# A hand-placed order for attention and a channel mixer on one core: new order lists, q of four pairs scaled on ScalarE, two more weight chunks split on GpSimd

## The chip, the cores and the metric

One core of a Trainium2 chip runs the whole program in one launch. The metric is the device time of the program in microseconds (us). Engines are named as in the profile: PE is TensorE's matmul and PEld its weight load, DVE is VectorE, ACT is ScalarE, POOL is GpSimd, SP is SyncE, which here only issues DMAs.

## What is computed

```python
def _attn_ref(q, k, v, tau):                     # q, k, v: 8 x 8 x 576 x 64, f32
    scores = np.matmul(q, k.transpose(0, 1, 3, 2)) / np.sqrt(64)
    thresh = np.max(scores, axis=-1, keepdims=True) - tau
    scores = np.where(scores >= thresh, scores, -1e9)
    scores = scores - np.max(scores, axis=-1, keepdims=True)
    attn = np.exp(scores)
    attn = attn / (np.sum(attn, axis=-1, keepdims=True) + 1e-09)
    return np.matmul(attn, v)

def _moe_ref(x, w_theta, w_tok_r, w_tok_i, w_ch):  # x: 8 x 576 x 512, the attention's output
    theta = x @ w_theta
    zr, zi = x * np.cos(theta), x * np.sin(theta)
    y = np.einsum('ts,bsd->btd', w_tok_r, zr) + np.einsum('ts,bsd->btd', w_tok_i, zi)
    u = x + y
    return u + np.maximum(u @ w_ch, 0.0)
```

## The kernel before, in words

**Work.** There are 8 batches with 4 pairs of heads each, 32 pairs in all, numbered n. A pair has five units (L782): a unit takes 128 queries of both heads (the fifth the last 64 of each) through the scores on PE (L800, into PSUM banks), a copy out of PSUM with the row's extreme on DVE (L821), the threshold (a small addition on DVE, L831), the mask and the exponential with its sum on ACT (L845, L852) and a transposition in 32x32 blocks on DVE (L864, L866) into the pair's one buffer `a`. When all five have been transposed, `values` (L870) multiplies `a` with v on PE in 32-row tiles, in two halves (L881), and `divide` (L901) divides by the sums, which go through DRAM to be spread over the partitions.

After the four pairs of a batch comes `mixture` (L954): four products with w_theta (`angle`, L1002; PE L989), sines and cosines on ACT (L1085 to L1092), products with x on POOL or DVE (L1107), transpositions on PE (`flip`, L1122; L1132) and splits into a high and a low part (ACT L1138, DVE L1157), four products with the token weights (`token`, L1165; PE L1177), and four products with w_ch (L989 again). Matmuls of the mixture, and from pair 5 on the scores, take each operand as a high and a low part of a faster number type, in three products.

**Weights.** At the start, and for w_ch after the first batch's angles, `convert` (L555) splits chunks of 128 weight rows into the two parts. The chunks have numbers, `turn`: 0 to 3 are w_theta, 4 to 12 the nine chunks of w_tok, 13 to 16 w_ch. Its steps run on ACT (L581), POOL or DVE (L586), DVE (L600, L607, L614), then the low word: for a turn under `WORD_POOL` (L617) a cast (L621) and a product (L626) on POOL, in two halves each, else one operation on DVE (L633). Three matmuls (L650 to L652) sum the pieces up, and ACT copies the low part out (L656).

**q.** From pair 5 on (`WHOLE`), q is scaled on DVE (L726) and split into parts (L735 or L737, and the subtraction of `low`, L533). Pairs 1 to 4 use q whole: a DMA, then one scaling in place on POOL (L713). Pair 0 is scaled while its scores are copied.

**Order.** Nothing in the source is run where it stands. Every operation is entered in a `Plan` (L367) with its engine, and a list `ORDER`, written into the source, says in which order they are issued: each number is the step from the last operation's number to the next one's. Operations are numbered as the source creates them. One engine's instructions run in the order of the list; between engines only semaphores order them. `PLACES` names the buffer (of the 2 to 8 of its class) that each tile takes. The costs at each operation (`c_mm`, `c_act`, ...) and the due times (`AT`, `key`) were the planner's when it made the list; at run time they have no effect. SP issues all loads and stores but the first, in the list's order.

Of the kernel before, what the change touches and what calls it, by code (L numbers as in the profile page):

```python
# [64 lines left out]
        "0101201010110202100121021000211021201210210221010210210210201212011201"  # L65
    ),
    "xl": (
        "001201021001210230101032112030123102330121023102320130213210301232103012310231023"
    ),
    "xh": (  # L70
        "10321001322310322301021301320112012301023102130123102310231203012320130123102310232013012320131023"
    ),
    "rb": (
        "010101100010010110010000001000100010011000000111"
    ),
    "bank": (
        "33223267764546646774760404044034404043040404500000055467544657764774657375646745766545767644400000700000"
        "04000000700000056774567464565436746547566646776656740000007000000600000060000007757665675476537467546457"
        "67675574767500000040000006000000600000046774564657647556564775467676765757640000007000000700000070000004"
        "67546754767543677674457466645646675700000060000005000000700000057665574674546775575466746545656774670000"  # L80
        "00600000060000007000000476567456724347567657774565676767574500000060000006000000500007463776246534567327"
        "334566772367324567"
    ),
    "z": (
        "1021210212001200120012001200120012001200101"
    ),
    "q": (
        "01012310213021302130213021302130213021302130213021302130213"
# [8 lines left out]
        "10231230231020310201230132012030321002311302101233203201232102103121032021032031012032110213022130102130"  # L97
        "13202130012302103012302301103201320012102301103210321230111023013202103102101230013203120232100132210310"
        "23110320123010320123012202102301321031201320012301230132003120120310213213010230"
    ),  # L100
    "nm": (
        "01210100120101020010021011001010010010101001010201201010101010010100121001001010010101001001010100101001"
        "01021001010010101001010210010100101010010200101001110100"
    ),
    "s2": (
        "01201012100120110202102012010001201100101001001201010101001010020010110101001101102011001010010100100112"
        "00120101010010101001001201010101000101010010100120010010"
    ),
    "rows": (
        "01001001010101010000010101010101"  # L110
# [5 lines left out]
        "01234560231450623145026431524063"  # L116
# [8 lines left out]
        "1023012301200213012010210132020101200120010201320123010201321203"  # L125
    ),
    "zl4": (
        "1023012301201203012301230132023101320123012301320123013201321302"
    ),
    "zh1": (  # L130
        "01010000010101010001010101000110"
    ),
    "zl1": (
        "01010001010101010101010101010110"
    ),
    "rawq": (
        "011010111001010101100101100"
# [164 lines left out]
WORD_POOL = 10  # L302
# [1051 lines left out]
```

## Time and profile before

| | us |
|---|---|
| median of 3 runs | 912.23 (912.0, 912.23, 917.48) |
| profiled execution | 910.66 |
| its span, first to last instruction | 908.9 |
| operations in the order list: PE, DVE, ACT, POOL, SP | 1370, 1244, 1040, 426, 292 |

The profile is of one execution. An engine is busy while one of its instructions runs; matmuls are pipelined and overlap, so a busy PE may still be slower than it could be. "Idle before" names what ended a pause of an engine, taken from the semaphores; "issue" is a pause that no semaphore explains. "L800" is line 800.

### The profile page before, as it was taken

To read this page: it belongs to the slowest core of one execution; us is meant where nothing else is said; L and a number is where in the kernel's file an instruction comes from. 1 tells how busy PE (TensorE), PEld (TensorE's weight loads), DVE (VectorE), ACT (ScalarE), POOL (GpSimd) and SP (SyncE) were. 2 spreads that over 40 slices of the span, in tenths; PEclk is the share of its full clock that TensorE was granted. 3 is DMA by queue.
4 is the path that set the end of the run, shared out by engine and by line. 5 is a ranking of instruction groups with operands and counts; after the bars stand their busy time and mean duration, and the time that the engine had idled before them with its cause. 6 is when DMAs were issued, how large, how long until landed. Compare 5 with 4: busy or idle time off the path is not lost.

```text
span 908.9 us, 33820 instructions
## 1 busy us (share of the span) xinstructions
PE 860.7 (95%) x14542; PEld 771.0 (85%) x14542; DVE 714.4 (79%) x1571; ACT 692.2 (76%) x1394; POOL 341.0 (38%) x432
## 2 busy tenths in 40 slices
PE   5787999999999989999999989999999999999898
PEld 3565898898998989888999979998889888999898
DVE  7999969988569887788788876788787886876452
ACT  6788998767987689766997679866888669975550
POOL 2677543133445234234432433534234433421210
PEclk9899999999999999999999999999999999999999
DMA  6576352465213644235233452415433352424502
GB/s 254 183 233 227 105 177 95 140 209 204 92 56 118 220 157 153 88 103 175 103 134 112 149 195 92 156 46 193 159 128 118 104 181 89 136 68 138 181 1 76
DMA packets 62374, 126.13 MB, mean 139 GB/s; under 512 B 22512, under 2 KB 31632, under 8 KB 58128
## 3 DMA queue, kind: packets, MB, share of 16 engines
q1 hardware_dynamic: 62080, 123.97, 40.6%
q8 instruction: 114, 1.87, 0.8%
q14 instruction: 36, 0.29, 0.1%
q10 hardware_dynamic: 144, 0.00, 0.0%
HBM read 110.17 MB, written 13.78 MB: 136 GB/s over the span
## 4 chain that ended last, share of the span: by engine, by line
PE 62%; DVE 23%; ACT 7%; issue 4%; DMA 2%; POOL 1%; SPq 1%; DVEq 0%; POOLq 0%; ACTq 0%
PE banks_ps__66 L1177 20%; PE banks_ps__66 L989 14%; PE banks_ps__66 L881 13%; PE banks_ps__66 L800 10%; DVE sc L821 8%; DVE a L864 4%; PE banks_ps__66 L1132 3%; ACT s L852 2%; ACT sc L845 2%; DVE nm L831 2%; DVE xl L533 1%; DVE xh L607 1%; DVE a L866 1%; ACT ang L1023 1%; PE banks_ps__66 L650 1%
## 5 line engine op out<-in xcount | busy, mean ns | idle before, releaser
L845 ACT ACTIVATE sc<-sc,nm 128x576 f32<-128x576 f32 x288 | 217.1, 771 | 78.3 <-DVE nm L831 75.5
L852 ACT ACTIVATE s<-sc,small 128x576 f32<-128x576 f32 x288 | 222.7, 774 | 5.0 <-DVE a L866 0.2
L821 DVE TENSOR_SCALAR_CACHE_REDUCE sc<-banks_ps__66 128x576 f32<-128x576 f32 x279 | 199.7, 743 | 13.2 <-PE banks_ps__66 L800 11.6
L864 DVE STREAM_TRANSPOSE a<-s 128x576 f32<-128x576 f32 x256 | 187.3, 758 | 26.4 <-PE banks_ps__66 L881 18.9
L800 PE MATMUL banks_ps__66<-k,q 64*128 64x288 f32 (+1 forms) x1638 | 176.6, 326 | 17.4 <-DVE sc L821 11.7
L881 PE MATMUL banks_ps__66<-a,v 32*64 32x144 f32 x9216 | 168.6, 288 | 12.8 <-issue 7.1
L989 PE MATMUL banks_ps__66<-xh,wm 128*128 128x288 f32 x1024 | 171.9, 304 | 3.7 <-issue 1.4
L800 PEld LDWEIGHTS banks_ps__66<-k,q 64*128 64x128 f32 (+1 forms) x1638 | 134.0, 188 | 45.6 <-DVE sc L821 22.6
L881 PEld LDWEIGHTS banks_ps__66<-a,v 32*64 32x64 f32 x9216 | 148.4, 132 | 27.2 <-issue 15.9
L1177 PE MATMUL banks_ps__66<-wt_h,zh 128*128 128x288 f32 x576 | 160.8, 304 | 0.9 <-ACT zh L1138 0.8
L1177 PE MATMUL banks_ps__66<-wt_l,zh 128*128 128x288 f32 x576 | 161.6, 303 | 0.0
L989 PEld LDWEIGHTS banks_ps__66<-xh,wm 128*128 128x128 f32 x1024 | 144.9, 190 | 17.2 <-issue 11.0
L1107 POOL TENSOR_TENSOR z<-z,xT 128x288 f32<-128x288 f32 x112 | 89.3, 832 | 100.8 <-ACT z L1088 100.8
L1177 PEld LDWEIGHTS banks_ps__66<-wt_h,zh 128*128 128x128 f32 x576 | 108.0, 189 | 4.2 <-issue 2.9
L1177 PEld LDWEIGHTS banks_ps__66<-wt_l,zh 128*128 128x128 f32 x576 | 108.3, 189 | 2.6 <-issue 2.3
L533 POOL TENSOR_TENSOR xl<-xT,xh 128x288 fp32r<-128x288 f32 x78 | 67.4, 886 | 98.8 <-ACT xh L948 39.5
L533 POOL TENSOR_TENSOR k<-rawk,k 128x288 fp32r<-128x288 f32 x54 | 47.5, 890 | 139.4 <-ACT k L763 69.8
L1177 PE MATMUL banks_ps__66<-wt_h,zl 128*128 128x288 f32 x576 | 96.6, 302 | 0.0
L989 PE MATMUL banks_ps__66<-xl,wm 128*128 128x288 f32 x512 | 94.2, 301 | 1.7 <-DVE xl L533 1.6
L1157 DVE TENSOR_TENSOR zl<-banks_ps__66,zh 128x512 fp32r<-128x512 f32 (+1 forms) x96 | 51.1, 548 | 50.9 <-ACT zh L1138 50.6
L533 POOL TENSOR_TENSOR q<-rawq,q 128x320 fp32r<-128x320 f32 x54 | 48.2, 906 | 97.9 <-ACT q L737 44.6
L1177 PEld LDWEIGHTS banks_ps__66<-wt_h,zl 128*128 128x128 f32 x576 | 81.7, 188 | 2.9 <-issue 2.7
(82 smaller groups left out, 1022.7 us busy)
## 6 DMA issues: line engine op xcount, KB each, us to landing
v<-in_vp_dram SPq DMA_DIRECT2D x32, 1152.0 KB
wm<-wm_dram SPq DMA_DIRECT2D x64, 512.0 KB
out_dram<-xT SPq DMA_DIRECT2D x31, 288.0 KB
rawq<-in_qT_dram SPq DMA_DIRECT2D x27, 320.0 KB
rb<-sums_dram SPq DMA_DIRECT2D x64, 128.0 KB
rawk<-in_kT_dram SPq DMA_DIRECT2D x27, 288.0 KB
z<-in_w_tok_dram SPq DMA_DIRECT2D x9, 576.0 KB
wm_dram<-rb SPq DMA_DIRECT2D x16, 256.0 KB
```

The lines of the kernel that those rows point to most:

```text
L533: eng.tensor_tensor(out=out()[:, c0:c1], in0=in0()[:, c0:c1], in1=in1()[:, c0:c1], op=ALU.subtract)
L800: nc.tensor.matmul(ps()[:, 2 * j + h, :HS], q[a]()[r, i * P : (i + 1) * P], k[c]()[r, h * HS : (h + 1) * HS], start=(x == 0), stop=(x == l ...
L821: lambda j=j, sc=sc, scaled=scaled: nc.vector.tensor_scalar(out=sc().rearrange("p (a b) -> p a b", a=2), in0=ps()[:, 2 * j : 2 * j + 2, :H ...
L845: lambda j=j, sc=sc: nc.scalar.activation(out=sc(), in_=sc(), func=AF.Prelu, bias=nm()[:, 2 + j : 3 + j], scale=-1.0, alpha=STEEP),
L852: lambda j=j, sc=sc, total=total, weights=weights: nc.scalar.activation(out=weights(), in_=keys(sc()), func=AF.Exp, bias=back, accum_out=p ...
L864: nc.vector.transpose(out=a()[:, :, j, 32 * i : 32 * i + 32], in_=src.rearrange("p (c q) -> p c q", q=32))
L881: nc.tensor.matmul(ps()[64 * h : 64 * h + 64, b, :w], v()[r, c, h, :], a()[r, c, h, :], start=(c == 0), stop=(c == 17))
L989: nc.tensor.matmul(ps[h]()[:, :HS], wm()[:, a, c, :], parts[c][bb]()[:, h * HS : (h + 1) * HS], start=first and n == 0, stop=final and n = ...
L1107: eng.tensor_tensor(out=zi, in0=zi, in1=x[m]()[:, c0:c1], op=ALU.mult)
L1132: nc.tensor.transpose(out=tp()[:, i * P : (i + 1) * P], in_=z()[:, c : c + P], identity=ident)
L1157: lambda zh=zh, zl=zl, tv=tv: nc.vector.tensor_tensor(out=zl(), in0=tv(), in1=zh().bitcast(F32), op=ALU.subtract),
L1177: nc.tensor.matmul(ps()[:, :HS], zz[c][lo]()[:, zz[c][2]], w[:, c, hs], start=(q + n == 0), stop=(q + n == len(work) - 1),)
```

## The change

PLACES and ORDER are replaced throughout; PLACES keeps its classes and sizes. `WORD_POOL` goes from 10 to 12, so turns 10 and 11 (the seventh and eighth chunk of w_tok) take their low words on POOL. The scaling of q of pairs 1 to 4 moves from POOL to ACT. A branch for the threshold's addition on ACT is added, which `ADD_ACT = 0` never takes. The new list has 1370, 1242, 1044, 430 and 292 operations.

```diff
 PLACES = {
     "wm": (
-        "0101201010110202100121021000211021201210210221010210210210201212011201"
+        "0101201201021020121020201212010210201201202012021002101201011221021021"
     ),
...
 ORDER = (
-    "202 1 -203 200 1 4 2 -206 205 -204 8 39 159 1 1 5 1*4 -202 -13 -1 2 1 207 12 1 25 -244 5 241 -32 14 -15 92 -90 "
...
 TWICE = 5
 WHOLE = 5
+ADD_ACT = 0
 HI_POOL = 8
-WORD_POOL = 10
+WORD_POOL = 12
...
             if n:
-                gps(
-                    c_pool(QS) * 0.5, lambda: nc.gpsimd.tensor_scalar(out=q(), in0=q(), scalar1=gate, scalar2=None, op0=ALU.mult), key,
+                act(
+                    c_act(QS, ptr=True), lambda: nc.scalar.activation(out=q(), in_=q(), func=AF.Copy, scale=gate), key,
                     ((q, 0), small_b), ((q, 0),),
                 )
...
         over = [(nm, list(heads)), small_b]
-        dve(
-            0.15,
-            lambda: nc.vector.tensor_scalar(out=nm()[:, 2 : 2 + w], in0=nm()[:, :w], scalar1=cut, scalar2=None, op0=ALU.add),
-            t0 + A("add", n), over, ((nm, 2),), small=True,
-        )
+        if n < ADD_ACT:
+            act(
+                0.22, lambda: nc.scalar.activation(out=nm()[:, 2 : 2 + w], in_=nm()[:, :w], func=AF.Identity, bias=cut),
+                t0 + A("add", n), over, ((nm, 2),),
+            )
+        else:
+            dve(
+                0.15,
+                lambda: nc.vector.tensor_scalar(out=nm()[:, 2 : 2 + w], in0=nm()[:, :w], scalar1=cut, scalar2=None, op0=ALU.add),
+                t0 + A("add", n), over, ((nm, 2),), small=True,
+            )
```

## Rows read from the trace of the kernel before

**Rows 1.** The page, busy time of each engine, share, instructions.
```profile
PE 860.7 (95%) x14542; PEld 771.0 (85%) x14542; DVE 714.4 (79%) x1571; ACT 692.2 (76%) x1394; POOL 341.0 (38%) x432
```
**Rows 2.** Stretches: length, busy us by engine, PE clock, DMA share, GB/s.
```profile
0.00:23.00 23.00, 12.58 (x54) 7.74 (x56) 16.95 (x47) 15.98 (x32) 6.11 (x14) 0.92 0.69 251
23.00:46.00 23.00, 17.68 (x429) 13.12 (x432) 22.04 (x49) 17.87 (x37) 14.68 (x23) 0.87 0.57 181
46.00:68.00 22.00, 19.29 (x377) 13.41 (x367) 21.40 (x46) 19.16 (x41) 15.48 (x24) 0.91 0.77 239
68.00:91.00 23.00, 17.92 (x327) 12.95 (x317) 22.83 (x48) 19.98 (x44) 16.32 (x27) 1.00 0.67 226
...
91.00:909.00 818.00, 793.21 (x13411) 723.83 (x13394) 631.22 (x1384) 619.20 (x1244) 288.42 (x346) 1.00 0.39 129
```
**Rows 3.** The page, chain that ended last, by engine.
```profile
PE 62%; DVE 23%; ACT 7%; issue 4%; DMA 2%; POOL 1%; SPq 1%; DVEq 0%; POOLq 0%; ACTq 0%
```
**Rows 4.** Waits of PE over the span: us, times, longest.
```profile
PE banks_ps__66 L800 <- DVE sc L821: 11.7, 10, 3.3
...
PE banks_ps__66 L881 <- issue: 7.1, 7, 2.1
...
PE banks_ps__66 L989 <- issue: 1.4, 1, 1.4
```
**Rows 5.** Timelines of PE and PEld (start, us, what, idle before), and chain.
```profile
425.46 0.49 PE L881 MATMUL banks_ps__66<-a,v 32*64 32x144 f32 x13 [1.10 <-issue]
...
517.78 0.83 PEld L800 LDWEIGHTS banks_ps__66<-k,q 64*128 64x128 f32 x12 [0.17 <-issue]
...
525.21 0.49 PE L881 MATMUL banks_ps__66<-a,v 32*64 32x144 f32 x10 [2.14 <-issue]
...
159.01 2.40 PE banks_ps__66 L1177 x18
161.42 2.44 PE banks_ps__66 L881 x144
```
**Rows 6.** DMA queue, kind, packets, MB, share of 16 engines.
```profile
q8 instruction: 114, 1.87, 0.8%
```
**Rows 7.** Groups by line: busy us, mean ns, idle before.
```profile
L713 POOL TENSOR_SCALAR q<-q,small 128x640 f32<-128x640 f32 x4 | 7.7, 1923 | 0.0
...
L737 ACT CAST q<-rawq 128x640 fp32r<-128x640 f32 x14 | 10.1, 725 | 0.0
...
L1088 ACT ACTIVATE z<-z,small 128x576 f32<-128x576 f32 x32 | 24.6, 770 | 0.2
...
L1090 ACT ACTIVATE z<-z 128x576 f32<-128x576 f32 x32 | 21.4, 669 | 0.0
...
L621 POOL CAST xh<-z 128x288 fp32r<-128x288 uint32 (+1 forms) x16 | 8.0, 498 | 1.8 <-PE banks_ps__66 L651 1.6 <-PE banks_ps__66 L650 0.2
...
L626 POOL TENSOR_TENSOR xh<-xh,xl 128x288 fp32r<-128x288 f32 (+1 forms) x20 | 16.4, 830 | 9.1 <-DVE xl L614 8.3 <-DVE nm L831 0.5
```
**Rows 8.** Timeline of PE, 16 to 23 us.
```profile
16.89 1.24 PE L800 MATMUL banks_ps__66<-k,q 64*128 64x288 f32 x8 [1.06 <-POOL q L713]
21.44 1.81 PE L800 MATMUL banks_ps__66<-k,q 64*128 64x288 f32 x6 [3.31 <-DVE sc L821]
```
**Rows 9.** Timelines of DVE and POOL, 91 to 99 us.
```profile
91.59 0.74 DVE L633 SCALAR_TENSOR_TENSOR xh<-z,xl 128x576 fp32r<-128x576 uint32 x1
...
93.71 0.79 DVE L633 SCALAR_TENSOR_TENSOR xh<-z,xl 128x576 fp32r<-128x576 uint32 x1
...
97.93 1.14 DVE L633 SCALAR_TENSOR_TENSOR xh<-z,xl 128x576 fp32r<-128x576 uint32 x1
...
96.52 0.95 POOL L533 TENSOR_TENSOR k<-rawk,k 128x288 fp32r<-128x288 f32 x1 [2.63 <-DVE k L761]
```
**Rows 10.** Stretches after the start-up, columns as in rows 2.
```profile
91.00:100.00 9.00, 9.00 (x279) 7.61 (x264) 8.42 (x17) 8.80 (x20) 3.98 (x5) 1.00 0.11 24
100.00:110.00 10.00, 9.06 (x57) 7.48 (x54) 9.93 (x21) 9.25 (x22) 8.58 (x10) 1.00 0.28 73
```

More of the change, by code (lines that the diff above doesn't have):

```diff
@@ L64 @@
     "wm": (
-        "0101201010110202100121021000211021201210210221010210210210201212011201"
+        "0101201201021020121020201212010210201201202012021002101201011221021021"
     ),
     "xl": (
-        "001201021001210230101032112030123102330121023102320130213210301232103012310231023"
+        "002132012001210232010120301231023012302130123103210233012102301321023310201320123"
     ),
     "xh": (
-        "10321001322310322301021301320112012301023102130123102310231203012320130123102310232013012320131023"
+        "10031212030321031302312002231013020123201312032013120302131203102312030123120301231023021312030123"
     ),
     "rb": (
-        "010101100010010110010000001000100010011000000111"
+        "010101010110010101010000011101110111010000100110"
     ),
     "bank": (
[L77 to L82, printed above, removed]
+        "33356732676565745767460044044430004402440404700000033276547655765774637567457447765746757467400000400000"
+        "05000000600000067646757647545667765756475546756646460000004000000700000040000004577465746452736546753576"
+        "44564747674500000050000007000000600000066774564765754766546677566446674675470000007000000300000050000006"
+        "67657476543256747654575676476746576400000050000004000000500000067664574675675646746765763456567646750000"
+        "00400000040000007000000467457657664457637465675674464765563600000070000004000000700003235673564323472367"
+        "352465577546733526"
     ),
     "z": (
-        "1021210212001200120012001200120012001200101"
+        "0210210201201200120012001200120012001200101"
     ),
     "q": (
-        "01012310213021302130213021302130213021302130213021302130213"
+        "01201312030120312031203120312013201230123012301230123012301"
     ),
@@ L96 @@
     "sc": (
-        "10231230231020310201230132012030321002311302101233203201232102103121032021032031012032110213022130102130"
-        "13202130012302103012302301103201320012102301103210321230111023013202103102101230013203120232100132210310"
-        "23110320123010320123012202102301321031201320012301230132003120120310213213010230"
+        "10102323120132003112300321303120123021033012310321023012031032021301032012300123031200123013200123130210"
+        "13202103102303102103202103012313021103201230012030123200123102120310231102312103012301203012301302010210"
+        "32101321031210021230123201021310320130221012023110320123001123012010230210310230"
     ),
     "nm": (
-        "01210100120101020010021011001010010010101001010201201010101010010100121001001010010101001001010100101001"
-        "01021001010010101001010210010100101010010200101001110100"
+        "00112012001010210010201010101201012010120101010010120101001010010210120101010010100102000120101010100101"
+        "02001010010100102001020110100101010101010100012001020010"
     ),
     "s2": (
-        "01201012100120110202102012010001201100101001001201010101001010020010110101001101102011001010010100100112"
-        "00120101010010101001001201010101000101010010100120010010"
+        "00112012001021001120102101002101101101011020110210100100101010001010120121001010011010120101120101020120"
+        "10110110121100100120101201101201001001101010011001010112"
     ),
     "rows": (
-        "01001001010101010000010101010101"
+        "01000010010100100101010000100010"
     ),
@@ L115 @@
     "xT": (
-        "01234560231450623145026431524063"
+        "01234560123540613524160532416052"
     ),
@@ L124 @@
     "zh4": (
-        "1023012301200213012010210132020101200120010201320123010201321203"
+        "0120102301200102012012010132013201230102010101200120213001020102"
     ),
     "zl4": (
-        "1023012301201203012301230132023101320123012301320123013201321302"
+        "0132012301230123012301230132013201230132012301230123103201320132"
     ),
     "zh1": (
-        "01010000010101010001010101000110"
+        "01010000010100010100000001010101"
     ),
     "zl1": (
-        "01010001010101010101010101010110"
+        "01010100010101010101010001010101"
     ),
     "rawq": (
-        "011010111001010101100101100"
+        "010100010101011001100000101"
     ),
```

259 rows, old and new, of the table ORDER are left out of this document.

## The prediction

> **What bounds the kernel now.** I read the busy shares first. TensorE (PE) is busy 95% of the span, VectorE (DVE) 79%, ScalarE (ACT) 76%, GpSimd (POOL) 38% [rows 1]. So the end is set by PE's work plus the time in which PE stands, and an engine beside PE counts only where PE waits for it. Where PE stands is read from the table by stretches [rows 2]. From 0 to 91 us PE is busy 12.58 + 17.68 + 19.29 + 17.92 = 67.5 us, so 23.5 us are idle; from 91 us to the end it is busy 793.21 of 818 us, so 24.8 us are idle. In the second to fourth of the early stretches DVE is busy 22.04 of 23, 21.40 of 22 and 22.83 of 23 us: the start-up is bound by DVE. The chain of work that ended last agrees: PE 62%, DVE 23%, ACT 7%, "issue" 4% [rows 3]. Last, the waits name what ends PE's idle time [rows 4]: 11.7 us end with DVE emptying a score bank, 8.5 us (7.1 in seven stops within the products with v, 1.4 in one elsewhere) end with "issue", that is with nothing the profile shows.
>
> The stops by "issue" are what the word "segments" in the change is about. In the timeline a half of 144 of these matmuls breaks off after 131, 1.10 us pass, and the last 13 follow with no other engine named; another half breaks off after 134 for 2.14 us [rows 5]. The queue marked "instruction" moved 114 packets and 1.87 MB [rows 6], 16.4 KB each; PE runs 14,542 matmuls and as many weight loads [rows 1], together 29,084, which is 113.6 times 256. So PE's program comes in 114 pieces of 256 instructions, and a piece can be late.
>
> **The change part by part.** The order lists can be counted without running anything: each step of ORDER is the number of the next operation in the order in which the source creates them.
>
> *Scaling q of pairs 1 to 4.* POOL loses 4 x 1.923 = 7.7 us [rows 7]. ACT gets four operations that no row shows. The nearest is its cast of the same 128x640 tile, 0.725 us; a pointer operand costs 0.10 us on the sine (0.770 against 0.669) [rows 7], so I take 0.83 each, 3.3 us in all. What it can give: in the one place where PE waited for this operation, 1.06 us [rows 8]. But 4.5 us later PE stands again, 3.31 us for DVE [rows 8], whose queue is no shorter. I take 0, with bounds of -1.1 us and of +3.3 us (all four in the way of the softmax; ACT is busy 53.0 of the first 68 us [rows 2], so it has room).
>
> *Words of two more chunks of w_tok on POOL.* DVE loses two operations, 0.74 and 0.79 us where they stood, at 91.6 and 93.7 us [rows 9]. POOL gets two casts (0.498 us each) and two products (0.830 us each) per chunk [rows 7], 5.3 us in all, so with the q scaling it is 2.4 us freer. The row of the stretch 91 to 100 us shows PE busy all of it, and 100 to 110 us shows DVE at 9.93 of 10 while PE is at 9.06 [rows 10], so DVE's gain reaches PE only there, and partly: I take half, -0.8 us. The bounds are -1.5 us and, if PE must wait for the slower words, +2.2 us: the casts need only the raw words and run early, but two products take 1.66 us in place of 0.77 us, 0.9 us more per chunk, and beside a busy POOL DVE itself is slower (1.14 us against 0.74 us for this very operation [rows 9]), 0.2 us more each.
>
> [...]
>
> *Pieces of 256.* Everything PE executes stays: 29,084 instructions in both lists. Changes of kind of tile (full, 64-row, 32-row, transposes) go from 553 to 547; at such a change the weight load is idle for 0.17 us [rows 5], so this is worth between nothing and 6 x 0.17 = 1.0 us, and I take -0.6 us. What moves is where the products with v lie. Each pair has 288 of these matmuls in two halves; between the halves the old order puts 2.8 us of other PE work on the mean (6.4 groups), the new one 1.9 us (4.2 groups). 144 of them take 2.44 us [rows 5], so a piece that holds nothing else lasts 2.17 us, and the two stops shown say that it then needs 2.17 + 1.10 = 3.3 us or 2.17 + 2.14 = 4.3 us until PE can go on. I cut both orders into pieces of 256, with the cuts where the stops of before lie, gave the other instructions 0.067 us each (18 full matmuls, with 18 weight loads, take 2.40 us [rows 5]), and summed what each piece after the start-up lacks of a need of 3.4 us: 15.7 us before, 12.4 us after (10.9 to 17.3 if the cuts shift by up to 20 instructions). The stops of before are 8.5 us, a share of 0.54, so this is worth -1.8 us. With a need of 4.0 us the same sum is 27.9 us before and 31.3 us after, worth +1.8 us: the new order has 24 pieces of 3.5 to 4.0 us where the old one has five. The typical stop is nearer to 3.4; I weight two to one and take -0.6 us. Bounds: -8.5 us (all stops gone) and +9.7 us (a need of 4.3 us: 35.1 to 44.8).
>
> *All other places.* On each engine an operation is moved by 2 to 3 us of work on the mean, SP's loads by the same, and the stages keep their places: after the second half of the products of pairs 7, 11, 15, ... PE has the same work left in both lists to within 1 us. So neither start-up nor tail is shortened by the order itself. What is drawn anew are the waits for DVE, ACT and POOL, 24.8 - 7.7 = 17.1 us after 91 us (the stops by issue after 91 us are 7.7). Reserves for those engines should make them fewer, but no row shows that; against it, PE's groups whose DVE operand stands less than its own duration ahead in the list rise from 61 to 79. I take -1.5 us, bounds -8 and +8.
>
> Sum: 0 - 0.8 - 0.6 - 0.6 - 1.5 = -3.5 us. The profiled execution took 910.66 us (span 908.9 and 1.8 us around it), so 907.2 us for such a one; it lies 1.6 us under the median of the runs, 912.23, so the median becomes 908.7 us, 0.4% less. A measurement of this kernel tells about 1% from no change.
>
> **Rivals.** *Faster: the stops vanish and the waits halve.* If the pieces are modelled rightly, the 7.7 us go, and half of the 17.1 us: -0.8 - 0.6 - 7.7 - 8.5 = -17.6 us, 894.6 us. For it: DVE has 21% and ACT 24% of idle time to be early in [rows 1]. Against it: the count leaves two thirds of the short pieces where they were. In part (over 9 us) I give it 0.26.
>
> *Slower: the halves of the products with v are too close.* Place: the cuts within pieces of 3.5 to 4.3 us, which the new order has in nearly every pair and the old one seldom. Price: 9.7 us if a piece needs 4.3 us, with the other terms but the third 912.2 - 2.9 + 9.7 = 919.0 us; if waits also grow by their bound of 8 us in place of falling, 928.5 us. It decides from a need of about 3.7 us on, where the gain of the short pieces is gone. For it: the stop of 2.14 us. Against it: seven of the eight stops are shorter. 0.24.
>
> *Words late on POOL.* PE waits for the two chunks, +2.2 in place of -0.8 us: 911.7 us, no change. For it: POOL's 2.66 us a chunk. Against it: POOL has waited 2.63 us when its next work comes there [rows 9]. 0.08. [...]
>
> *The order does not do what it says:* stops and waits are as many as before, elsewhere, with the second part's -0.8 us alone 911.4 us. 0.12. The rest, 0.30, is the forecast, 904 to 911 us.
>
> **How the numbers follow.** The forecast and the two rivals of no change lie within 1%, and so does half of the slower one: 0.30 + 0.08 + 0.12 + 0.06 = 0.56; faster 0.26, slower 0.18. The range leaves out what goes beyond 897 us (near all of the faster rival) and beyond 921 us (the slower rival with more waits).
>
> **What would show it.** Right: the idle rows by "issue" within the products with v total 5 to 9 us; PE idle 21 to 24 us up to 91 us; no PE wait for ACT's q; DVE 1.5 us less busy, ACT about 3.3 us more, POOL about 2.4 us less. Wrong: "issue" above 12 us (the need is nearer to 4 us), or PE's idle time after 91 us below 15 us (the order was worth more), or a new row in which PE waits for POOL's words or low parts.

## The result, and the profile after

| | before | after |
|---|---|---|
| median of 6 runs, us | 912.12 (911.63 to 917.48) | 923.9 (917.52 to 927.0) |
| profiled execution, its span, us | 910.66, 908.9 | 917.52, 915.7 |

The ratio of the means is 1.0106 with a 95% interval from 1.0075 to 1.0138: the kernel after is 1.1% slower, and the forecast of 908.7 us was wrong in sign. The profiled execution after is the fastest of its six, so its rows account for 6.8 of the 11.8 us between the medians; the six granted clocks (means of 0.983 to 0.987, the profiled one's 0.985) leave some 2 us at the most of the rest to the clock, and where the remainder went no profile shows.

The page of the kernel after has the busy time of each engine, the instruction queue and the chain that ended last:

```profile
PE 866.3 (95%) x14542; PEld 775.4 (85%) x14542; DVE 708.9 (77%) x1569; ACT 696.3 (76%) x1398; POOL 339.7 (37%) x436
...
q8 instruction: 114, 1.87, 0.9%
...
PE 67%; DVE 17%; ACT 7%; issue 4%; DMA 2%; POOL 2%; SPq 0%; DVEq 0%; POOLq 0%; ACTq 0%
```

Against [rows 1, 3, 6] the instructions of PE and the 114 pieces are the same, DVE's part of the chain fell from 23 to 17%, and PE is busy 5.6 us longer with the same instructions. That last number is the first hint of TensorE's clock, which the profiles of the two kernels show at two levels alone: 1.00 and 0.50 of the whole (after, 440 to 446 and 433 to 439 us).

The waits of PE in the kernel after (us, times, longest), from 91 to 338 us and behind:

```profile
PE banks_ps__66 L890 <- issue: 5.2, 5, 2.2
PE banks_ps__66 L1186 <- issue: 1.8, 2, 1.3
PE banks_ps__66 L803 <- issue: 1.0, 1, 1.0
...
PE banks_ps__66 L890 <- issue: 7.5, 5, 3.5
PE banks_ps__66 L803 <- DVE sc L824: 2.2, 4, 0.8
```

The same views of the kernel before:

```profile
PE banks_ps__66 L800 <- DVE sc L821: 3.2, 4, 2.1
...
PE banks_ps__66 L881 <- issue: 0.2, 1, 0.2
...
PE banks_ps__66 L881 <- issue: 6.1, 5, 2.1
```

The first three rows after add up to 8.0 us of stops by "issue" where there were 0.2; behind 338 us there are 7.5 in both (before, with the 1.4 us of [rows 4] that lie there). All rows of this kind that name DVE fall from 11.5 to 5.8 us after 91 us. So the reserves, the lead that the new order gives the other engines over PE, shortened these waits, and 8 us of stops at late pieces between 91 and 338 us took it back.

The rest is the clock. The windows of 425 to 447 us, with PE's granted clock (1.00 is the higher level) in the third column from the end, after and then before:

```profile
425.00:447.00 22.00, 18.53 (x275) 16.33 (x259) 15.10 (x29) 14.22 (x32) 9.13 (x10) 0.84 0.40 127
```
```profile
425.00:447.00 22.00, 21.30 (x307) 19.30 (x307) 20.45 (x45) 18.92 (x39) 6.94 (x8) 1.00 0.40 146
```

The timeline of PE after (start, us, what, idle before) at that stop, and around 248 us:

```profile
427.99 2.27 PE L890 MATMUL banks_ps__66<-a,v 32*64 32x144 f32 x128
433.73 0.79 PE L890 MATMUL banks_ps__66<-a,v 32*64 32x144 f32 x16 [3.47 <-issue]
...
247.14 0.44 PE L1186 MATMUL banks_ps__66<-wt_h,zh 128*128 128x288 f32 x1
247.38 0.44 PE L1186 MATMUL banks_ps__66<-wt_l,zh 128*128 128x288 f32 x1
...
248.55 0.29 PE L1186 MATMUL banks_ps__66<-wt_l,zh 128*128 128x288 f32 x1
248.68 0.30 PE L1186 MATMUL banks_ps__66<-wt_h,zh 128*128 128x288 f32 x1
```

The half of the products with v that began at 427.99 us breaks off after 128 matmuls for 3.47 us, and 6.8 us at the lower clock level (0.50) begin in this stop, 1.2 us before its end. What that level costs is seen at 247 and 248.6 us: the same matmuls follow each other every 0.24 us in a half-clock stretch and every 0.13 us right behind it. Such stretches last 3.4 or 6.8 us; after 30 us they hold 10.2 us before and 20.4 us after, and where PE works each us of them gives about half of it away.

The bill of the two profiled executions, after 91 us: stops +7.8, waits for DVE -5.7, clock +5.1 (an estimate, half of the 10.2 us that the kernel after has more), together +7.2 us; the spans differ by 6.8. The bill leaves out 0.9 us more of waits for ACT and POOL and counts 0.6 us twice, for the clock in a stop costs nothing. PE's row of the windows after 91 us, beside the last of [rows 2], agrees in kind: PE is idle 26.9 us of 825 where it was 24.8 of 818, and busy 4.9 us longer:

```profile
91.00:916.00 825.00, 798.08 (x13442) 727.30 (x13433) 629.28 (x1384) 619.95 (x1242) 293.04 (x353) 0.99 0.40 130
```

### The profile page after: what moved, and what is told of

Its sections match the earlier page's. It is cut to its first block, busy times and chain, and to the rows that moved or that the text cites. A ratio compares the mean times of both kernels' runs of the same rounds, so it can differ in the third digit from the quotient of the medians.

```text
span 915.7 us, 33839 instructions
## 1 busy us (share of the span) xinstructions
PE 866.3 (95%) x14542; PEld 775.4 (85%) x14542; DVE 708.9 (77%) x1569; ACT 696.3 (76%) x1398; POOL 339.7 (37%) x436
## 4 chain that ended last, share of the span: by engine, by line
PE 67%; DVE 17%; ACT 7%; issue 4%; DMA 2%; POOL 2%; SPq 0%; DVEq 0%; POOLq 0%; ACTq 0%
PE banks_ps__66 L1186 23%; PE banks_ps__66 L998 15%; PE banks_ps__66 L890 14%; PE banks_ps__66 L803 11%; DVE sc L824 5%; DVE a L873 4%; PE banks_ps__66 L1141 3%; ACT s L861 2%; ACT sc L854 2%; DVE nm L840 1%; ACT ang L1032 1%; POOL xl L536 1%; DVE xh L610 1%; DMA wm<-in_w_theta_dram 1%; ACT ang L1018 1%
## 5 line engine op out<-in xcount | busy, mean ns | idle before, releaser
L803 PE MATMUL banks_ps__66<-k,q 64*128 64x288 f32 (+1 forms) x1638 | 177.2, 328 | 18.1 <-DVE sc L824 11.5
L890 PE MATMUL banks_ps__66<-a,v 32*64 32x144 f32 x9216 | 171.8, 290 | 16.0 <-issue 13.5
```

The costliest lines, as they stand in the source:

```text
L803: nc.tensor.matmul(ps()[:, 2 * j + h, :HS], q[a]()[r, i * P : (i + 1) * P], k[c]()[r, h * HS : (h + 1) * HS], start=(x == 0), stop=(x == l ...
L890: nc.tensor.matmul(ps()[64 * h : 64 * h + 64, b, :w], v()[r, c, h, :], a()[r, c, h, :], start=(c == 0), stop=(c == 17))
```

## Experiments

The theory was first A, that late pieces make the difference (B: the new order itself makes PE wait longer), then its sharper form A'', that the loads running when a piece is requested make it late. The tables give the ratio to the kernel before, run beside it, with its interval, PE's stops by "issue" from 91 to 338 us and behind (8.0 and 7.5 after, 0.2 and 7.5 before), PE's waits for DVE after 91 us (5.8 after, 11.5 before), and the half-clock time from 90 us on but for the last few us of the span (13.6 after, 3.4 before), each from the profile of one execution of that kernel, while the ratio is over all of them.

### Moving the cuts between pieces

Small matmuls ahead of all work shift the cuts through the order and change nothing else (5, 28, 20 and 5 of them, of 4 instructions each):

```diff
+        for _ in range(5):
+            nc.tensor.matmul(psum[:32, 7, :4], ident[:, :32], ident[:, :4], start=True, stop=True)
         plan.run()
```

> The changed kernel with 20 tiny PE instructions ahead of everything (5 matmuls of 4 columns), which shift every cut into pieces of 256 by 20 instructions and change no order. Theory A (late pieces make the change slow): counted on the trace of the changed kernel, what the pieces lack of 3.4 us falls from 13.6 to 11.0 us and pieces shorter than 2.5 us from 10 to 4, so the stops by issue on PE fall from 16.4 us to 8 to 11 us, with fewer stretches at the lower clock, and the time falls to 912 to 919 us, ratio to the kernel before 1.000 to 1.007. Theory B (the new order itself makes PE wait longer for other engines): no change, ratio 1.008 to 1.013.

> The changed kernel with 112 tiny PE instructions ahead (28 matmuls of 4 columns, some 3 to 5 us where PE waits for its first load anyway). Theory A: the pieces lack 21.7 us of 3.4 us in place of 13.6, so stops by issue rise by 4 to 8 us and more stretches at the lower clock follow: 929 to 940 us, ratio 1.018 to 1.03. Theory B: no change beyond 1 us, ratio 1.008 to 1.014.

> The kernel before with 80 tiny PE instructions ahead (20 matmuls of 4 columns). Theory A: the pieces lack 18.4 us in place of 14.6, stops by issue 10 to 13 us in place of 8.5, and perhaps one more stretch at the lower clock: 914 to 918 us, ratio 1.002 to 1.007. Theory B: no change, ratio 0.998 to 1.002.

> The kernel before with 20 tiny PE instructions ahead, the control. Theory A: the pieces lack 15.1 us in place of 14.6, stops by issue 8 to 10 us, 911 to 914 us. Theory B: the same, 911 to 914 us. If this one moves by more than 0.4%, the added matmuls do something else (to the clock at the start, say).

| | ratio | stops | DVE | half clock |
|---|---|---|---|---|
| after_cut20 | 1.0103 [1.004, 1.0166] | 11.7, 4.7 | 5.1 | 13.6 |
| after_cut112 | 1.0075 [1.005, 1.0101] | 6.8, 12.7 | 4.5 | 10.2 |
| before_cut80 | 1.0021 [1.0001, 1.0041] | 7.1, 3.6 | 10.9 | 10.2 |
| before_cut20 | 0.9997 [0.9975, 1.0019] | 2.5, 7.3 | 10.2 | 3.4 |

The stops go to other instructions with the cuts, up to 4.6 us at one place, while the waits for DVE stay with the order. So the stops are the cuts, and the shorter waits belong to the order. A count over all 20 profiles of this study says it without exception: with all of PE's instructions on the trace (the matmuls, weight loads and semaphore instructions, and the drain that is first) numbered from 0 in their order, each of the 164 stops by "issue" of over 0.5 us stands where the number leaves 193 or 194 when divided by 256. The sizes expected from one need of 3.4 us for every piece missed in the kernel after, where the cut that should have been best gained nothing, and after_cut112, from which 1.8% or more was expected, is 0.75% slower; before_cut80 and before_cut20 came out as expected in ratio and stops.

The trace says why. It has the packet of each piece and the instruction at which PE enters the piece ahead of it, which I take for the moment when the packet is asked for. A stop is then the delay until the packet starts, plus its transfer, plus 1.4 us (1.2 to 1.6) until PE goes on, less the time that the piece in between lasts; over the 20 profiles this gives 148 of the 151 stops of over 0.5 us behind 89 us to 0.2 us, and the other three to 0.23. The transfer takes 0.9 to 1.8 us at these stops. The delay is not fixed. Over ten profiles (before, after and the runs of this part and the next, with after_quarter_v), where a piece of under 4.2 us was running, it is 0.45 us on the mean when the DMA engines were less than a tenth busy in the 2 us behind the request, and 2.1 us when they were over nine tenths busy. How busy they were in the 2 us ahead of it says little (0.63 against 0.79 us). At the 3.47 us stop above the delay is 3.4 us. The DMA view of 427 to 432 us of the kernel after, with the busy tenths of the 16 engines, shows what is under way:

```profile
DMA  1739911917346999999779997999978999797400
...
q1 hardware_dynamic: 615, 1.36, 81.2%
q8 instruction: 1, 0.02, 1.3%
...
wm<-wm_dram SPq DMA_DIRECT2D x1, 512.0 KB
```

In the kernel before, 27 pieces behind 20 us lasted under 4.2 us, and the delay of the packet asked for at their start was 0.59 us on the mean; at 6 of these requests a reload of wm had been issued in the last 5 us. After, there are 42, the delay is 0.93 us, and 14 of them meet such a reload. With one need for all, the pieces of the two kernels would lack nearly the same, 9.8 us after and 9.3 before at a need of 3.1 us, and no further apart than 2.1 us at any need tried from 2.9 to 4.3 us; with the need that each met, 17.0 against 8.6 us.

Loads are not all of the delay. Of the eight stops of 0.9 us or more after 91 us in the kernel after, the two that end at 99.43 and 619.84 us had a delay of 1.1 and 1.5 us with the engines idle, and at 348.0 us of before_spread (of the next part) a request was followed by 5.0 us without its packet, the engines idle too, and a stop of 1.39 us. What made these late is open.

### Moving the halves of the products with v

Only the two halves of pairs 4 to 31 move in PE's order, by at most four groups in the first two kernels; in the third the second half alone is pulled forward. The first of some 50 to 90 edits of ORDER in each, in the order of the labels below:

```diff
-    "... -313 1 298 -284 1 -32 314 2 7 -322 ..."
+    "... -313 1 298 -284 -31 314 2 7 -291 ..."
...
-    "... -285 1 296 1 -6 40 -330 -11 -6 1 ..."
+    "... -285 1 296 1 34 -330 290 -301 -6 1 ..."
...
-    "... 6 -5 6 -37 18 292 1 -292 1 ..."
+    "... 6 -5 6 -37 315 -297 292 1 -292 1 ..."
```

> The kernel after with the halves of the products with v of pairs 4 to 31 moved by at most four groups of TensorE's order; every other instruction keeps its place among the others, the mean of other TensorE work between the two halves of a pair goes from 2.0 to 2.8 us, and the count of tile-mode changes stays within a few. By the order and the rows' durations, what the segments of 256 fall short of 4.2 us adds up to 40 us in the kernel after, 32 in the kernel before and 24 in this one. Theory A (late instruction segments: a segment needs some 3.5 us with idle DMA engines and 4 to 7 us where data fills them, and stops of over 2 us cost a half-clock stretch besides): stops of TensorE for instructions after 91 us 5 to 10 us instead of 15.6, half-clock stretches after 30 us 7 to 14 us instead of 20, time 905 to 914 us, not slower than the kernel before. Theory B (the new order as a whole, its waits for other engines or its pauses, whatever the places of the halves): 917 to 926 us, ratio to the kernel before 1.006 to 1.013, stops as they fall.

> The kernel before with the halves of the products with v of pairs 4 to 31 moved by at most four groups of TensorE's order; what the segments fall short of 4.2 us adds up to 20 us instead of 32. Theory A: stops for instructions after 91 us 3 to 6 us instead of 8 to 11, waits for VectorE 11 to 13 us as before, time 3 to 8 us under the kernel before of the same call (ratio 0.991 to 0.997). Theory B: ratio 0.998 to 1.002.

> The kernel before, with only the second half of the products with v of pairs 4 to 31 pulled forward, so that the mean of other TensorE work between the two halves goes from 3.0 to 1.8 us, as in the kernel after. What the segments fall short of 4.2 us adds up to 47 us instead of 32. Theory A: stops for instructions after 91 us 13 to 19 us instead of 8 to 11, more half-clock stretches (14 to 24 us), ratio to the kernel before 1.006 to 1.016, though q scaling, words and the rest of the order are those of before. Theory B: ratio 0.998 to 1.003.

| | ratio | stops | DVE |
|---|---|---|---|
| after_spread | 1.0606 [1.0567, 1.0646] | 7.6, 7.4 | 29.1 |
| before_spread | 1.0575 [1.0534, 1.0617] | 2.2, 5.5 | 38.3 |
| before_close | 1.0402 [1.036, 1.0444] | 0.2, 7.6 | 24.8 |

Every expectation missed. The waits of PE in after_spread, over its span:

```profile
PE banks_ps__66 L887 <- DVE sc L821: 8.3, 13, 1.6
PE banks_ps__66 L918 <- DVE rows L914: 6.2, 4, 3.0
...
PE banks_ps__66 L995 <- POOL xl L533: 3.7, 6, 1.2
```

Rows like these are small or missing before and after: the other engines keep their order, and their results now come too late for PE. The test cannot say what the spacing alone is worth: in before_close, with a span 38 us longer, PE is idle 20 us more after 91 us and busy 18 us more (some 12 of them, by an estimate, at the lower clock), and its stops by "issue" are those of before. It shows how little of a balanced order can be moved.

### Undoing the two small parts

q of pairs 1 to 4 back on POOL, and the words of turns 10 and 11 back on DVE, at the places of the new order:

```diff
-                act(
-                    c_act(QS, ptr=True), lambda: nc.scalar.activation(out=q(), in_=q(), func=AF.Copy, scale=gate), key,
+                gps(
+                    c_pool(QS) * 0.5, lambda: nc.gpsimd.tensor_scalar(out=q(), in0=q(), scalar1=gate, scalar2=None, op0=ALU.mult), key,
```
```diff
             for i in range(2):
+                if turn >= 10:
+                    gps(0.1, lambda: None, key, (raw,), ((w, i),))
+                    gps(0.1, (lambda: nc.vector.scalar_tensor_tensor(
+                        out=w()[:, :n], in0=lb(), scalar=1.0, in1=mb().bitcast(F32), op0=ALU.mult, op1=ALU.mult
+                    )) if i else lambda: None, key, ((w, i), mag), ((w, i),))
+                    continue
```

> The kernel after with the scaling of q of pairs 1 to 4 back on GpSimd, at the same places of the order. If the scaling costs nothing on either engine, as in the sum of the prediction: within 0.2% of the kernel after (ratio to the kernel before 1.006 to 1.014), the wait of TensorE for q at the start 1.0 us instead of 0.7. If ScalarE's four instructions of 1.9 us are what the new order pays for: 3 us or more less than the kernel after.

> The kernel after with the word products of the two conversions that the change moved to GpSimd back on VectorE, one instruction each instead of four, issued where GpSimd's last piece stood. If the shorter waits of TensorE for VectorE (5.7 us after 91 us, 12.0 in the kernel before) are owed to the order, they stay at 5 to 7.5 us and the time within 0.3% of the kernel after (ratio to the kernel before 1.006 to 1.015). If they are owed to the 5.5 us that VectorE has less to do, they go back to 9 us or more.

| | ratio | stops | DVE | half clock |
|---|---|---|---|---|
| after_q_on_pool | 1.0116 [1.0079, 1.0154] | 8.4, 9.9 | 6.7 | 13.6 |
| after_words_on_dve | 1.0085 [1.0066, 1.0104] | 11.0, 7.1 | 4.7 | 13.6 |

Both stay at the kernel after, and the waits for DVE stay short. (The four instructions on ACT take 0.82 us each; the 1.9 us in the expectation are POOL's.) Neither part by itself is the cause, and the new order with its places carries both the gain and the loss.

### Taking the loads away

These kernels issue the same operations in the same order, but after the first load into a buffer the later ones carry only a quarter of the bytes: v (in after_quarter_v alone with one buffer for all pairs, so that each load also waits for the last use); wm from the third block on; then v, wm, rawq, rawk and the spread sums (two DMAs in place of four), mostly behind 330 us; then these from the start on; last, the writes of wm_dram too. The buffers keep older numbers, so later results are made of other numbers. The loads of v, wm, rawq (rawk alike) and the spread sums, and the writes, with `full` true at the first load into a buffer:

```diff
-            nc.sync.dma_start(v().rearrange("p c h d -> p (c h d)"), src)
+            w = 18 * 2 * D // (1 if v.full else 4)
+            nc.sync.dma_start(to[:, :w], src[:, :w])
...
-        load(lambda: nc.sync.dma_start(t().bitcast(F32), wm_dram[which, m]), key, (wm_b[which],), (t,), 512)
+            w = 2 * NM * P if t.full else NM * P // 2
+            nc.sync.dma_start(to[:, :w], src[:, :w])
...
-            load(lambda r=r: nc.sync.dma_start(raw()[:, r], qT[n // NP, n % NP][:, r]), k + A("raw", n), (), ((raw, i),), w // 2)
+            load(lambda r=r: (raw(), nc.sync.dma_start(raw()[:, : QS if full() else QS // 4], qT[n // NP, n % NP][:, : QS if full() else QS // 4])), k + A("raw", n), (), ((raw, i),), w // 2)
...
+                if not rc.full:
+                    nc.sync.dma_start(rc()[r, 0:128], flat[:, 640 * j : 640 * j + 128].broadcast_to([64, 128]))
+                    nc.sync.dma_start(rc()[r, 512:528], last[j][:1].broadcast_to([64, 64 // parts]))
+                    continue
...
-                        wm_dram[which, :, :, i, c, :].rearrange("m p e -> p m e"),
-                        t()[:, :DM].bitcast(F32).rearrange("p (m e) -> p m e", e=P),
+                        wm_dram[which, :1, :, i, c, :].rearrange("m p e -> p m e"),
+                        t()[:, :P].bitcast(F32).rearrange("p (m e) -> p m e", e=P),
```

> The kernel after with the load of v cut to the first quarter of its columns for pairs 1 to 31 (the rest of v stays that of pair 0, so the products with v are made of other numbers; instructions and order are the same). 288 KB instead of 1152 KB then cross the DMA engines right behind each second half. Theory A in the form that DMA load sets how late a segment is: stops after 91 us 6 to 11 us instead of 15.6, the delay from the request of a segment to its start at the same places 0.6 to 1.3 us where it was 1.5 to 3, time 907 to 916 us. Rival (a segment's need is fixed, or set by other transfers): stops 13 to 18 us at the same places as in the kernel after, time 916 to 925 us.

> The kernel after with the reloads of wm (the weights of the channel products, 512 KB each) cut to the first quarter of each partition's bytes from the third block of four pairs on, but for the first into each of the buffers (the rest of wm stays what that buffer held, so later channel products are made of other numbers); instructions and order are the same. Theory A'': a segment's need is the delay from its request to its start, its transfer and 1.4 us; in the kernel after the requests that belong to short segments (under 4.2 us: 41, against 24 before) fall into reloads of wm at 21 of 41 (7 of 24 before), and their mean delay is 1.12 us against 0.57. With the reloads cut, that delay falls to 0.5 to 0.8 us from 300 us on, stops of TensorE for instructions after 91 us to 8 to 12 us instead of 15.6, time 909 to 917 us, within 0.5% of the kernel before with the same cut on either side. Rival (the number of short segments alone decides, or something outside the DMA engines): stops 14 to 20 us, ratio to the kernel before 1.008 to 1.014 as for the kernel after.

> The kernel before with the same cut of the reloads of wm (later channel products are made of other numbers). Theory A'': few of its short segments are requested in a reload of wm, so stops go from 8 to 11 us to 6 to 9 us, and the time to 0.994 to 1.000 of the kernel before. Rival (the transfers cost everywhere alike): it gains as much as the kernel after does from the cut, and the 1% between the two stays.

> The kernel after with most of its reloads cut to a quarter: v (1152 KB) from pair 1, wm (512 KB) from the third block, rawq, rawk and the spread sums (320, 288 and 128 KB) from pair 12, each but for the first into each buffer (the rest of each buffer keeps older numbers, so later pairs and blocks are made of other numbers); instructions and order are the same but for the number of DMAs of the spread sums (two instead of four). Theory A'': with a need that is the same for all segments, 2.9 to 3.1 us (1.4 after landing, 1.1 transfer, 0.4 to 0.6 delay where no load is under way), the segments of the kernel after fall short by 8 to 10 us in all, those of the kernel before by 9 to 12; so with few loads the kernel after loses its late segments (stops after 91 us 6 to 10 us instead of 15.6), keeps its shorter waits for VectorE (5 to 7 us against 11 to 13), and is as fast as the kernel before with the same cut or faster: 1 to 8 us under it, 904 to 910 us. Rival (the loads are not what makes them late; the number of short segments or something else of the new order does): stops 13 us or more and 5 us or more above the kernel before with the same cut.

> The kernel before with the same cut of the reloads (later pairs and blocks are made of other numbers). Its short segments were requested where few loads ran, so theory A'' expects little: stops after 91 us 6 to 10 us (7.9 in the profile of before), waits for VectorE 11 to 13 us, ratio to the kernel before 0.992 to 1.000. Rival: the same, so that the comparison with the kernel after of the same cut decides.

> As after_light_loads, with the same reloads cut from the start on: every reload of wm and v and of the spread sums but the first into a buffer, rawq and rawk from pair 5 (later pairs and blocks are made of other numbers). In after_light_loads the stops behind 338 us, where all these loads were cut, fell from 7.7 to 3.0 us (those of before_light_loads to 4.5), and between 91 and 338 us, where most still ran, they stayed (11.1 us against 8.0 in the kernel after). Theory A'': between 91 and 338 us the stops now fall to 2 to 5 us too (the writes of wm_dram and the loads of the weights stay), the half-clock time after 91 us to 7 us or less, and the kernel is as fast as the kernel before with the same cut or faster, by 0 to 7 us: ratio to the kernel before 0.985 to 0.995. Rival (something else of the new order in that stretch): 7 us or more of stops stay there, ratio 0.998 to 1.004.

> The same cut in the kernel before. Theory A'': stops of 0 to 1.5 us between 91 and 338 us and of 4 to 5 us behind, waits for VectorE 11 to 13 us after 91 us, ratio to the kernel before 0.990 to 0.997. Rival: the same; the comparison with the kernel after of the same cut decides.

> As after_light_early, and the 16 writes of the converted weights into wm_dram cut to the first of the four m too, 64 KB instead of 256 KB (all reloads then read that one, so the channel products are made of other numbers). In after_light_early the largest stop left, 3.2 us at 98.2 us, belongs to a segment that was requested 0.1 us after such a write was issued and started 3.0 us later; half-clock stretches of 6.8 us began beside it, and the kernel still was 0.4% over before_light_early (stops of 10.7 against 4.6 us, waits for VectorE 5.1 against 12.3, half-clock time after 91 us 10.2 against none). Theory A'': that stop falls to 1.5 us or less and the half-clock time beside it goes: stops 6 to 9 us after 91 us, half-clock time after 91 us 0 to 4 us, time 2.5 to 6 us under after_light_early (ratio to the kernel before 0.991 to 0.996) and within 0.25% of the kernel before with the same cut. Rival (what is left is not the loads): within 0.15% of after_light_early, 0.4% above before_light_writes.

> The same cut in the kernel before, where the last of the first eight writes is issued at 66 us (90.7 us in the kernel after) and no large stop follows one. Both: within 0.2% of before_light_early (ratio to the kernel before 0.991 to 0.996).

| | ratio | stops | DVE | half clock |
|---|---|---|---|---|
| after_quarter_v | 1.013 [1.0081, 1.0179] | 12.4, 8.2 | 7.7 | 10.2 |
| after_quarter_wm | 1.0056 [1.0029, 1.0082] | 9.1, 4.1 | 7.1 | 20.4 |
| before_quarter_wm | 0.9967 [0.995, 0.9985] | 1.2, 6.4 | 11.7 | 3.4 |
| after_light_loads | 1.0009 [0.9991, 1.0027] | 10.9, 3.0 | 5.8 | 10.2 |
| before_light_loads | 0.9944 [0.9927, 0.9962] | 1.1, 4.4 | 12.1 | 0 |
| after_light_early | 0.9982 [0.9967, 0.9998] | 6.3, 4.2 | 4.2 | 10.2 |
| before_light_early | 0.9938 [0.9914, 0.9961] | 1.5, 2.9 | 12.1 | 0 |
| after_light_writes | 0.9977 [0.9952, 1.0002] | 8.7, 2.9 | 6.3 | 3.4 |
| before_light_writes | 0.9958 [0.9941, 0.9974] | 1.4, 4.4 | 11.6 | 0 |

The reload of v, which my first reading held to be the cause because it follows each second half, is not by these rows: the stops stayed (two executions). Without most of wm the kernel after gains 0.5% and the one before 0.3%, so 0.9% stay between them where A'' expected 0.5% at most: this test came out as its rival said. With all reloads light, the kernel after comes down by 1.0 to 1.3%, the one before by 0.4 to 0.6%, and the 1.1% between them shrinks to 0.65, 0.44 and 0.19% (quotients of the ratios). So by the last two pairs more than half of the loss needs the loads; the intervals, some 0.3% either way, are wide for that. The stops themselves do not follow as clearly: between the kernels of such a pair they differ by 8.4, 6.1 and 5.8 us, and uncut by 7.8; what shrank beside them, in the last pair, is the surplus of half-clock time, from 10.2 to 3.4 us. The waits of PE behind 338 us, where after_light_loads is light, and between 91 and 338 us, where it mostly is not:

```profile
PE banks_ps__66 L922 <- issue: 3.0, 3, 1.3
...
PE banks_ps__66 L922 <- issue: 7.2, 4, 2.6
PE banks_ps__66 L835 <- issue: 2.7, 1, 2.7
PE banks_ps__66 L1223 <- issue: 1.0, 1, 1.0
```

And before_light_loads behind 338 us:

```profile
PE banks_ps__66 L913 <- issue: 3.8, 7, 1.4
```

The stops fell where the loads were taken (7.5 to 3.0, and in the kernel before 7.5 to 4.4) and nowhere else. But A'' expected after_light_loads to be as fast as before_light_loads, and it met the rival's terms, 13 us of stops and 5 us above it. And A'' said that after_light_early would have 2 to 5 us of stops between 91 and 338 us and be at or under before_light_early. It had 6.3 us and was not, and its largest stop, 3.2 us, stands at 98 us. The timeline of PE's products with v there, in the kernel after:

```profile
90.82 4.12 PE L890 MATMUL banks_ps__66<-a,v 32*64 32x144 f32 x140 [0.95 <-DVE a L875]
95.70 2.25 PE L890 MATMUL banks_ps__66<-a,v 32*64 32x144 f32 x128 [0.76 <-issue]
99.43 0.71 PE L890 MATMUL banks_ps__66<-a,v 32*64 32x144 f32 x20 [1.47 <-issue]
```

And in the kernel before:

```profile
90.19 2.44 PE L881 MATMUL banks_ps__66<-a,v 32*64 32x144 f32 x136 [0.80 <-DVE sc L821]
...
95.87 2.51 PE L881 MATMUL banks_ps__66<-a,v 32*64 32x144 f32 x144
```

The DMA share is in the last column but one of the windows of 91 to 103 us, of the kernels before, after and after_light_early in this order:

```profile
91.00:103.00 12.00, 11.35 (x290) 9.26 (x274) 11.39 (x24) 11.11 (x25) 6.98 (x9) 1.00 0.27 71
```
```profile
91.00:103.00 12.00, 9.76 (x304) 8.49 (x297) 8.16 (x18) 9.45 (x18) 8.85 (x12) 0.86 0.57 150
```
```profile
91.00:103.00 12.00, 7.53 (x291) 6.83 (x289) 8.06 (x21) 8.71 (x16) 9.88 (x15) 0.77 0.43 116
```

After, both halves of a pair stand back to back, 140 + 128 + 20 = 288 matmuls, more than two pieces in a row (the middle row is one piece, 2.25 us), and beside loads and a write of wm_dram; PE is busy 9.76 of 12 us. Before, 3.2 us of other work lie between the halves and the DMA engines are half as busy. Even a piece that meets idle DMA engines needs 2.9 us (0.4 + 1.1 + 1.4, an estimate from the means above), so two of 2.25 us stop PE whatever the loads do. This is the one place where the rival's words are true to the letter. Cutting the write of wm_dram did not remove the stops (2.2 us at 96 us and 3.4 at 102 us in after_light_writes), so that step of the last expectation fell, and the time fell by 0.05% where 2.5 us or more were expected, although the two kernels came within the 0.25% it named; between the last two cuts the intervals overlap, and 0.44 and 0.19% cannot be told apart. That the rest of the difference is owed to these two pieces is argued from the rows, not shown: I did not move one of the two halves alone, nor a load within the order.

Of the kernels that compute the same as the one before, none beats it; before_cut20 equals it.

## Why the prediction was wrong

**What bounds the kernel:** right, as far as it went. The bill of PE's pauses and clock comes within 0.4 us of the difference of the spans.

**Scaling q:** 0 forecast, and after_q_on_pool shows no difference from the kernel after. The row after is:

```profile
L716 ACT ACTIVATE q<-q,small 128x640 f32<-128x640 f32 x4 | 3.3, 816 | 0.0
```

That is 0.82 us each where 0.83 was estimated. The sign "no PE wait for ACT's q" failed in a harmless way, as the timeline after shows:

```profile
16.91 1.24 PE L803 MATMUL banks_ps__66<-k,q 64*128 64x288 f32 x8 [0.74 <-ACT q L716]
21.37 3.25 PE L803 MATMUL banks_ps__66<-k,q 64*128 64x288 f32 x12 [3.22 <-DVE sc L824]
```

PE waits 0.74 in place of 1.06 us, and the 3.31 us for DVE behind it [rows 8] are still 3.22: what was gained in one wait did not come through the next.

**Words on POOL:** not settled. By the ratios the kernel after is 0.2% (1.9 us) slower than after_words_on_dve, and the interval of that difference, some 0.4% either way, holds both the -0.8 us and the bound of +2.2. By the rows of before POOL takes 3.4 times as long as DVE for the low word of a chunk (2.66 against 0.77 us); the product alone is 2.2 times (1.66 us), and the rest is the cast, which POOL does in an operation of its own.

**All other places:** -1.5 with bounds of 8; measured -5.7 us in the waits for DVE, -4.8 with those for ACT and POOL. The mechanism was named and undersized. That the new order's reserves halved the waits for DVE could not be read from the trace of before. PE's idle time up to 91 us came to 22.75 us, within the 21 to 24 forecast. DVE is 5.5 us less busy where 1.5 was forecast.

**Pieces of 256:** the step that failed. The prediction weighed needs of 3.4 and 4.0 us two to one and took -0.6 us for the fetch; the stops grew by 7.8 us, most of the 9.7 us of the rival "the halves of the products with v are too close". The prediction's own sign of being wrong, "issue" above 12 us, came: 16.3 us over the span. Its count saw the danger, 24 pieces of 3.5 to 4.0 us where the old order has five (19 and 5 on the traces, behind 20 us). What it had wrong was the form: there is no one need of a piece, and on the traces none would have told the two orders apart by more than 2.1 us. The need is 1.4 us, a transfer of about 1.1 us and a delay between nothing and 4.6 us beside a short piece, which grows with the loads under way (0.45 to 2.1 us on the mean). The stop of 2.14 us of the kernel before [rows 5] was evidence for this, with a delay of 2.1 us beside a reload of wm; I read it as the odd one of eight. A better sum would have put each short piece's request beside the loads that the new order issues there, not beside a constant.

**The clock** was in no term, and no reason was given for leaving it out. It costs about 5 us by the estimate above, as much as all that the reserves gained, and belongs to the price of the stops: of the three half-clock stretches of the kernel after behind 91 us, those at 244.8 and 432.5 us begin just behind and in stops of 2.23 and 3.47 us; the one at 91.2 us and the only one of the kernel before, at 323.0 us, follow waits for DVE. By these numbers a stop of 3 us is worth 4.7 where a half-clock stretch of 3.4 us follows.

The range ended at 921 us, between the slower rival and its case with more waits. That this rival with the clock's price on top, 919 + 5 = 924 us, is the median is chance: the 5 us were read in an execution of 917.5 us, and its stops and waits differ from the rival's terms (+7.8 for +9.7, -4.8 for -1.5).

## What to carry to other kernels

Where a program has bursts of some hundred small matmuls, count PE's instructions in blocks (of 256 here) and look at what the DMA engines do in the microseconds after a block is asked for, one block ahead; a short block (here one under 4.2 us) wants quiet DMA engines at its start (a delay of 0.45 against 2.1 us here). A plan that gives every block the same fetch time can look alike on paper (9.8 against 9.3 us here) where the stops differ by a factor of two. Price a pause of PE with the clock that may follow it (4.7 us for a stop of 3 here, by the estimate above), and test a hand-made order by moving as little as possible: a few groups moved cost 4 to 6%.

## What the runs showed of the hardware

The profile counts the pieces of 16.4 KB (q8) and the loads (q1) on the same 16 DMA engines, 1.3 and 81.2% of them from 427 to 432 us in the kernel after, and the wait for a piece was at times longer than its transfer of 0.9 to 1.8 us: 4.6 us from request to start was the longest beside a short piece (after_cut112, 640 us), 0.38 us the mean where no DMA had been issued in the 5 us before (14 requests beside short pieces in the kernel after). That a piece holds 256 instructions is read from the 164 stops above and from the 114 packets for 29,084 matmuls and weight loads, and on the traces of the two kernels 114 instructions have a number that leaves 194 when divided by 256, one for each packet.

Over the 20 profiles of this study PE paused 51 times for more than 1.8 us after 90 us, and a half-clock stretch began during the pause or close behind it 36 times. Every such stretch from 90 us on, but those at the end of a run, had pauses of PE close ahead of it, and not at late pieces alone: the one of the kernel before follows a wait of 2.08 us for DVE. That the pauses are its cause is what the rows suggest; no run here set pauses without changing something else.
